# Recutting the head of a fused attention and MLP kernel

## The chip, the cores and the metric

The kernel runs on one core of one Trainium2 chip. The metric is the device time of one execution in microseconds (us); the runs before the change have a median of 356.44 us.

## The reference

Attention over 8 batches and 8 heads, 576 tokens of 64 features, with 16 extra "beacon" keys and values in front that every query sees; the rest is causal. The result, as 4608 tokens of 512 features, goes through a two-layer MLP with a leaky ReLU.

```python
k_all = np.concatenate([beacon_k, k], axis=2)
v_all = np.concatenate([beacon_v, v], axis=2)
scores = (1 / np.sqrt(D)) * np.matmul(q, k_all.transpose(0, 1, 3, 2))
scores = np.where(causal, -1e9, scores)      # causal only among the 576 own keys
a = softmax(scores)
x = np.matmul(a, v_all)                      # (B, H, S, D) -> (B*S, H*D)
h = x @ w_in                                 # 4608 x 512 @ 512 x 2048
out = np.maximum(0.01 * h, h) @ w_out        # 2048 x 512
```

## The kernel before

The work is cut into 32 groups, one for each pair of heads of a batch: group g is pair g % 4 of batch g // 4. Every engine's queue is written out by hand, in the order of the Python code (`tc.manual_schedule`), so each engine runs its instructions strictly in that order, and what the code puts earlier stands earlier in the queue of its engine.

For a group the steps are: queries and keys with features on the partitions (`qT`, `kT`); `score`, in four parts, each of which fills one of two PSUM buffers (`ps_sc`), with ScalarE's exponential behind it into `aT` (three buffers, `a_bufs`); `masks`, four GpSimd selects that clear what lies above the diagonal; `value`, in two halves, the product with v and the division by the row sum (VectorE); and `finish`, five transposes that put the result into `xT`, from which the MLP reads. `value` runs two groups behind `score`, and `finish` three.

The MLP is cut into "groups" of its own: `moe1` (four matmuls of 512 columns, then ScalarE's leaky ReLU into `gT`) and `moe2` (four matmuls of the second layer; every fourth is copied out by VectorE and stored by SP). `fill()` issues the next one whose inputs are there. They fill TensorE between the steps of attention.

The keys and queries come in two ways. For the first two batches (groups 0 to 7) they are loaded by GpSimd's DMA with a cast to bf16 (`load_qk`), turned by TensorE (`t_q`, 18 transposes of 64 x 64 for each of q and k) and copied from PSUM by VectorE or ScalarE. The very first pair is loaded in fp32 by SP and ScalarE (`load_first_pair`) and cast by VectorE and ScalarE (`first_cast`). From batch 2 on, GpSimd permutes them (`permute`), a transposing DMA turns them (`turn_pairs`, on SP's queue) and GpSimd copies them into order (`in_order`, a beacon column block of 16, then q, then k). Each `kT` buffer has 16 beacon columns in front; they are copied from `bkT`, which `beacon_transposes` fills from the cast beacon keys (`cast_beacon_k`). There are two `kT` buffers (`k_bufs`).

v comes in fp32 by SP in five chunks a batch (`load_v`), after the first keys have landed, and is cast by GpSimd (`cast_v`) into `v_aug`. The weights come by GpSimd's DMA with a cast, w_in and w_out in four quarters each, between groups 3 and 6 (`loads`). At the very start TensorE runs 34 matmuls on the identity (`warm_up`).

The main loop `for g in range(NG + 3)` has two forms: groups 0 to 7 (the head) follow a fixed list, with a special stretch at g = 8 that works off what is left of batches 0 and 1, runs 22 MLP groups, and loads batch 2; from there on MLP groups are spread over eight slots in each iteration. Work of GpSimd for later batches is put into `loads(g)`.

Of the kernel before, what the change touches and what calls it, by code (L numbers as in the profile page):

```python
# [15 lines left out]
def kernel(  # L16
# [11 lines left out]
    nc = tc.nc  # L28
# [69 lines left out]
    k_bufs = [singles.tile([128, NKB * 128], BF16, name=f"kT{i}") for i in range(2)]  # L98
# [9 lines left out]
    def load_w_in(i):  # L108
        return nc.gpsimd.dma_start(
            out=w_in_sb[:, :, i * 512 : (i + 1) * 512], in_=w_in_r[:, :, i * 512 : (i + 1) * 512]  # L110
        )

    def load_w_out(i):
        return nc.gpsimd.dma_start(
            out=w_out_sb[:, i * 4 : (i + 1) * 4, :], in_=w_out_r[:, i * 4 : (i + 1) * 4, :]
        )
# [5 lines left out]
    def load_qk(b, grp):  # L122


        qk_raw[b, grp] = (
            qkpool.tile([128, 2, RI, D], BF16, name="q_raw"),
            qkpool.tile([128, 2, RI, D], BF16, name="k_raw"),
        )
        first = None
        for e in range(2):  # L130
            if b == 0 and grp == 0 and e == 0:
                continue
            h0 = 4 * grp + 2 * e
            for src, dst in zip((q, k), qk_raw[b, grp]):
                dma = nc.gpsimd.dma_start(  # L135
                    out=dst[e * RP : (e + 1) * RP],
                    in_=src[b, h0 : h0 + 2].rearrange("h (p i) d -> p h i d", i=RI),
                )
                first = first or dma
        return first  # L140
# [3 lines left out]
    def load_first_pair():  # L144
        load_beacon_k(0, 1, nc.scalar)
        t = rawpool.tile([128, NKB, H, D], FP32, name="v_raw")
        flat = t[0:RP].rearrange("p c h d -> p (c h d)")
        n = 2 * RI * D
        for i in range(2):
            first_raw.append(flat[:, i * n : (i + 1) * n].rearrange("p (h i d) -> p h i d", h=2, i=RI))  # L150
        for eng, src, dst in zip((nc.sync, nc.scalar), (q, k), first_raw):
            last = eng.dma_start(out=dst, in_=src[0, 0:2].rearrange("h (p i) d -> p h i d", i=RI))
        return last

    first_cast = [singles.tile([RP, 2, RI, D], BF16, name=f"{n}_cast") for n in "qk"]
# [26 lines left out]
    def beacon_transposes(b0, b1):  # L182
# [6 lines left out]
        for par in range(2):  # L189
            ps_ = slice(par * 64, par * 64 + 64)  # L190
            nc.vector.tensor_copy(
# [35 lines left out]

    def t_q(g, which, copy=nc.vector.tensor_copy):
# [4 lines left out]
        if which == 0:  # L233
            dst = headpool.tile([128, S], BF16, name="qT")
            qk[g] = [dst]
        else:
            kT = k_bufs[g % 2]
            nc.vector.tensor_copy(out=kT[:, 0:NB], in_=bkT[:, b, hp])
            qk[g].append(kT)
            dst = kT[:, NB : NB + S]  # L240
# [28 lines left out]
    def in_order(g):  # L269
# [4 lines left out]
        kT = k_bufs[g % 2]  # L274
# [11 lines left out]
    def score(g, n):  # L286
# [21 lines left out]
        )  # L308

# [130 lines left out]
    def warm_up(n):  # L440

        ps = ps_one.tile([128, 512], FP32, name="av", tag="one")
        for i in range(n):
            nc.tensor.matmul(out=ps[:, 0:128], lhsT=ident, rhs=ident, start=True, stop=True)
# [15 lines left out]
    with order:  # L460
# [4 lines left out]
        load_beacon_k(1, B, nc.sync)  # L465
        load_v(0, after=first)
        load_v(1)
        make_pads()
        make_ones()
        cast_beacon_k(0, 1, nc.scalar.copy)  # L470
        nc.vector.tensor_copy(out=first_cast[0], in_=first_raw[0])
        nc.scalar.copy(out=first_cast[1], in_=first_raw[1])
        cast_beacon_k(1, B, nc.gpsimd.tensor_copy)
        cast_v(0, nc.gpsimd, 0, 1)
        load_qk(1, 0)
        cast_v(0, nc.gpsimd, 1, 3)
        warm_up(34)
        beacon_transposes(0, 1)
        t_q(0, 0)
        t_q(0, 1, nc.scalar.copy)  # L480

        def loads(g):
            b, hp = divmod(g, NPAIR)
            if g == 1:
                cast_v(0, nc.gpsimd, 3, 5)
            elif g == 2:
                load_qk(1, 1)
            elif g == 3:
                cast_v(1, nc.gpsimd, 0, 3)
                load_w_in(0)  # L490
            elif g == 4:
                cast_v(1, nc.gpsimd, 3, 5)
                load_w_in(1)
                load_w_in(2)
            elif g == 5:
                load_w_in(3)
                load_w_out(0)
                load_w_out(1)
            elif g == 6:
                load_w_out(2)  # L500
                load_w_out(3)
            elif g == 7:
                load_qk(2, 0)
            elif g >= 2 * NPAIR:
                if has(g + 1):
# [28 lines left out]
        for g in range(NG + 3):  # L534
# [3 lines left out]
            if g < 2 * NPAIR:  # L538
# [3 lines left out]
                if has(g - 3):  # L542
                    finish(g - 3)
                if g == 2:
                    beacon_transposes(1, B)
                if g + 1 < 2 * NPAIR:
                    t_q(g + 1, 0)
                    t_q(g + 1, 1, nc.scalar.copy if g in (4, 6) else nc.vector.tensor_copy)
                if g > 2:
                    value(g - 2, 0)  # L550
                if g == 7:
                    fill()
                score(g, 2)
                score(g, 3)
                if g == 2:
                    value(0, 0)
                if g >= 6:
                    fill()
                if has(g - 2):
                    value(g - 2, 1)  # L560
                masks(g)
                continue

            if g == 2 * NPAIR:
# [6 lines left out]
                load_v(2)  # L571
                in_order(g)
                cast_v(2, nc.gpsimd)
# [85 lines left out]
```

The softmax here doesn't subtract the row's maximum and nothing guards it: scores larger than these inputs give would overflow.

## Time and profile before

| what | value |
|---|---|
| median of 4 runs | 356.44 us (355.56 to 357.4) |
| profiled execution, its own time | 356.41 us |
| span of that execution, first to last instruction | 354.7 us |
| busy: TensorE | 341.0 us (96%) |
| busy: ScalarE | 189.1 us (53%) |
| busy: GpSimd | 202.0 us (57%) |
| busy: VectorE | 92.8 us (26%) |
| mean granted TensorE clock | 0.980 |
| first exponential starts | 8.77 us |
| first exponential of group 7 starts | 37.14 us |
| block of 22 MLP groups starts | 48.42 us |

PE is TensorE's matmuls, PEld its weight loads, DVE is VectorE, ACT ScalarE, POOL GpSimd, SP SyncE; ACTq, SPq and POOLq are the queues on which DMAs are issued. A row of the timeline gives start and duration in us, engine, line, operation, output and inputs, how many, and in brackets how long the engine was idle before it and what ended that. In a row of stages the numbers behind the window are the window's length and then, for each engine, busy us and the number of instructions; then the granted clock as a share of full speed, the busy share of the DMA engines and what they moved.

### The profile page before, as it was taken

How to read it: one execution, taken by the hardware profiler on the slowest of the kernel's cores; microseconds unless marked ns; L12 is line 12 of the kernel's file. 1: busy time of each engine (PE TensorE's matmuls, PEld its weight loads, DVE VectorE, ACT ScalarE, POOL GpSimd, SP SyncE). 2: the span in 40 equal slices, each digit the busy share in tenths (PEclk: the TensorE clock that was granted, in tenths of full speed). 3: DMA queues.
4: the chain of work that ended last, by engine and by line, in shares of the span. 5: the costliest groups of instructions: out<-in, count | busy, mean ns of one | idle time of the engine just before them, and what ended most of it. 6: DMA issues, size and time to landing. Idle time of an engine off the chain costs nothing.

```text
span 354.7 us, 7340 instructions
## 1 busy us (share of the span) xinstructions
PE 341.0 (96%) x3002; PEld 173.1 (49%) x3002; DVE 92.8 (26%) x231; ACT 189.1 (53%) x278; POOL 202.0 (57%) x343
## 2 busy tenths in 40 slices
PE   6899999998899999999999999999999999999996
PEld 5566554443454454444444454444444554444444
DVE  2478420002233223222222223222322241000111
ACT  3969754576455873478337843685358403633300
POOL 6699927399899899957695769574431100000000
PEclk9579999999999999999999999999999999999999
DMA  8999999997797976991589356900110011000012
GB/s 170 209 198 161 194 204 187 224 217 124 163 198 114 174 146 125 136 234 31 97 148 225 56 98 114 177 2 1 61 59 2 0 62 59 2 30 30 31 60 88
DMA packets 86929, 40.87 MB, mean 115 GB/s; under 512 B 69872, under 2 KB 82160, under 8 KB 86896
## 3 DMA queue, kind: packets, MB, share of 16 engines
q1 hardware_dynamic: 73456, 26.75, 35.2%
q0 software_dynamic: 13152, 13.34, 24.8%
q8 instruction: 23, 0.38, 0.5%
q10 hardware_dynamic: 288, 0.33, 0.4%
q14 instruction: 10, 0.08, 0.1%
HBM read 37.22 MB, written 9.44 MB: 132 GB/s over the span
## 4 chain that ended last, share of the span: by engine, by line
PE 73%; DMA 11%; POOL 9%; issue 2%; DVE 2%; SPq 1%; ACT 1%; POOLq 0%; ACTq 0%
PE acc L409 32%; PE acc L387 27%; PE av L351 7%; PE sc L297 6%; DMA v_raw<-in_v_dram 4%; DMA w_out_sb<-in_moe_w_out_dram 4%; POOL aT L320 3%; DMA q_raw<-in_q_dram 2%; PE tp L373 2%; DMA v_raw<-in_k_dram 1%; POOL v_aug L224 1%; DVE osb L418 1%; POOL qT L277 1%; POOL kT L277 1%; POOL k_raw L135 1%
## 5 line engine op out<-in xcount | busy, mean ns | idle before, releaser
L387 PE MATMUL acc<-xT,w_in_sb 128*128 128x512 bf16 x576 | 140.2, 379 | 1.4 <-DVE xT L378 1.4
L409 PE MATMUL acc<-w_out_sb,gT 128*128 128x512 bf16 (+1 forms) x592 | 139.6, 374 | 0.0
L306 ACT ACTIVATE aT<-sc 128x1024 bf16<-128x1024 f32 (+3 forms) x128 | 104.2, 869 | 64.7 <-PE sc L297 63.3
L394 ACT ACTIVATE gT<-acc 128x512 bf16<-128x512 f32 x144 | 85.9, 601 | 79.2 <-PE acc L387 79.2
L409 PEld LDWEIGHTS <-gT 128*128 128x128 bf16 x592 | 53.3, 98 | 58.7 <-issue 6.1
L320 POOL TENSOR_SCALAR_AFFINE_SELECT aT<-aT 128x384 bf16<-128x384 bf16 (+2 forms) x128 | 52.5, 448 | 50.2 <-PE av L351 40.3
L387 PEld LDWEIGHTS <-w_in_sb 128*128 128x128 bf16 x576 | 51.9, 98 | 59.5 <-issue 4.2
L418 DVE COPY osb<-acc 128x512 f32<-128x512 f32 (+1 forms) x37 | 25.1, 677 | 134.7 <-PE acc L409 134.6
L351 PEld LDWEIGHTS <-aT 128*128 128x128 bf16 (+1 forms) x960 | 37.5, 99 | 14.7 <-issue 2.6
L297 PE MATMUL sc<-qT,kT 64*128 64x80 bf16 (+4 forms) x384 | 37.1, 295 | 5.5 <-POOL kT L277 2.4
L351 PE MATMUL av<-v_aug,aT 128*128 128x65 bf16 (+1 forms) x960 | 40.7, 196 | 0.0
L361 DVE TENSOR_TENSOR x_nat<-av,rec 128x384 bf16<-128x384 f32 x64 | 31.4, 491 | 2.2
L224 POOL CAST v_aug<-v_raw 128x512 bf16<-128x512 f32 (+1 forms) x40 | 23.3, 616 | 9.6 <-DMA v_raw<-in_v_dram 9.5
L297 PEld LDWEIGHTS <-kT 64*128 64x128 bf16 x384 | 12.9, 96 | 31.3 <-issue 18.7
L277 POOL COPY qT<-q_turn 128x576 bf16<-128x576 bf16 x24 | 28.1, 1171 | 0.0
L277 POOL COPY kT<-k_turn 128x576 bf16<-128x576 bf16 x24 | 28.0, 1167 | 0.0
L378 DVE COPY xT<-tp 128x576 bf16<-128x576 bf16 x32 | 14.5, 455 | 50.9 <-PE tp L373 50.9
L360 DVE RECIPROCAL rec<-av 128x6 f32<-128x6 f32 x64 | 12.0, 187 | 59.2 <-PE av L351 59.2
L135 POOL DMA_DIRECT2D k_raw<-in_k_dram x31 | 19.6, 632 | 4.6 <-DMA w_out_sb<-in_moe_w_out_dram 3.9
L135 POOL DMA_DIRECT2D q_raw<-in_q_dram x31 | 19.0, 613 | 2.7 <-DMA w_out_sb<-in_moe_w_out_dram 2.5
L164 POOL COPY q_nat<-q_raw 128x1152 bf16<-128x1152 bf16 x12 | 13.7, 1145 | 5.5 <-DMA q_raw<-in_q_dram 5.4
L373 PEld LDWEIGHTS <-x_nat 128*128 128x128 bf16 (+2 forms) x160 | 11.2, 98 | 8.8 <-DVE x_nat L361 1.7
(36 smaller groups left out, 85.0 us busy)
## 6 DMA issues: line engine op xcount, KB each, us to landing
out_dram<-osb SPq DMA_DIRECT2D x35, 256.0 KB, 2.3
v_raw<-in_v_dram SPq DMA_DIRECT2D x24, 256.0 KB, 5.1
q_raw<-in_q_dram POOLq DMA_DIRECT2D x31, 144.0 KB, 5.1
k_raw<-in_k_dram POOLq DMA_DIRECT2D x31, 144.0 KB, 5.4
w_in_sb<-in_moe_w_in_dram POOLq DMA_DIRECT2D x4, 512.0 KB, 7.9
w_out_sb<-in_moe_w_out_dram POOLq DMA_DIRECT2D x4, 512.0 KB, 13.1
v_raw<-in_v_dram SPq DMA_DIRECT2D x8, 224.0 KB, 3.6
v_raw<-in_v_dram SPq DMA_DIRECT2D x8, 160.0 KB, 5.0
```

The costliest lines, as they stand in the source:

```text
L135: dma = nc.gpsimd.dma_start(out=dst[e * RP : (e + 1) * RP], in_=src[b, h0 : h0 + 2].rearrange("h (p i) d -> p h i d", i=RI),)
L224: eng.tensor_copy(out=dst[0 : ROWS[c], c, :, 0:D], in_=t[0 : ROWS[c], c])
L277: nc.gpsimd.tensor_copy(out=dst.rearrange("c (p i) -> c p i", i=RI), in_=t[:, :, e].rearrange("c i p -> c p i"),)
L297: nc.tensor.matmul(out=sc[:, par, col - c0 : col - c0 + w], lhsT=kT[ps_, c * 128 : (c + 1) * 128], rhs=qT[ps_, q0 : q0 + w], start=True, s ...
L306: nc.scalar.activation(out=aT[:, :, c0 : c0 + w], in_=sc[:, :, 0:w], func=AF.Exp, scale=0.125)
L320: nc.gpsimd.affine_select(out=part, in_=part, compare_op=ALU.is_ge, fill=0.0, base=base, channel_multiplier=-1, pattern=pattern,)
L351: nc.tensor.matmul(out=avv[:, n, 0 : D + 1], lhsT=aT[0 : ROWS[c], par, a0 : a0 + 128], rhs=va[0 : ROWS[c], c, 2 * hp + par, :], start=(c = ...
L361: nc.vector.tensor_tensor(out=x_nat[:, t0:t1].rearrange("p t e d -> p (t e) d"), in0=avv[:, :, 0:D], in1=rec[:, n0:n1, None].to_broadcast( ...
L387: nc.tensor.matmul(out=acc, lhsT=w_in_sb[:, j, fc * 128 : (fc + 1) * 128], rhs=xT[:, j, i * 512 : (i + 1) * 512], start=(j == 0), stop=(j ...
L394: nc.scalar.activation(out=gT[i][:, fc, :], in_=acc, func=AF.Prelu, alpha=0.01)
L409: nc.tensor.matmul(out=acc[:, 0:w], lhsT=gT[i][:, fc, t * 128 : (t + 1) * 128], rhs=w_out_sb[:, fc, c0 : c0 + w], start=(fc == 0), stop=(f ...
L418: nc.vector.tensor_copy(out=osb[:, 0:w], in_=acc[:, 0:w])
```

## The change

- ScalarE's queue issues the first keys' DMA first and the beacon keys' DMA second; that load takes two batches instead of one. The other six are loaded by SP behind v of batch 1, cast by GpSimd in group 6, and transposed at g = 8.
- The first keys are cast half by ScalarE and half by VectorE, into buffers of the pool for q_nat and k_nat; the beacon's cast, transposes, and columns for groups 0 and 1 stand ahead of these casts.
- The 34 identity matmuls become 24, 12, 6 and 10, spread over the start, and 12 in each of groups 0 and 1.
- In the head, `score` parts 0 and 1 are followed at once by the next group's transposes, and `finish` goes to the end of the iteration. MLP groups are taken out of group 6; one is in group 7, and one more in front of g = 8.
- The beacon columns of groups 2 to 7 are copied by GpSimd instead of VectorE; there are three `kT` buffers.
- Group 0 is masked by VectorE, by multiplying with a triangle of ones that GpSimd makes once.
- v of batch 0 is cast earlier in GpSimd's queue; loads of q and k of batch 1 are cut by pair and issued a little later; each weight comes in two halves, issued in groups 4 to 6.
- `in_order(9)` moves from `loads(8)` to g = 8, ahead of `cast_v(2)`.

```diff
-    k_bufs = [singles.tile([128, NKB * 128], BF16, name=f"kT{i}") for i in range(2)]
+    k_bufs = [singles.tile([128, NKB * 128], BF16, name=f"kT{i}") for i in range(3)]
...
+    def load_w_in(half):
+        cols = slice(half * DF // 2, (half + 1) * DF // 2)
+        return nc.gpsimd.dma_start(out=w_in_sb[:, :, cols], in_=w_in_r[:, :, cols])
+
+    def load_w_out(half):
+        rows = slice(half * NF // 2, (half + 1) * NF // 2)
+        return nc.gpsimd.dma_start(out=w_out_sb[:, rows, :], in_=w_out_r[:, rows, :])
...
     def load_first_pair():
-        load_beacon_k(0, 1, nc.scalar)
...
             last = eng.dma_start(out=dst, in_=src[0, 0:2].rearrange("h (p i) d -> p h i d", i=RI))
+        load_beacon_k(0, 2, nc.scalar)
         return last
...
+    def beacon_columns(g, eng):
+        b, hp = divmod(g, NPAIR)
+        eng.tensor_copy(out=k_bufs[g % 3][:, 0:NB], in_=bkT[:, b, hp])
...
-            kT = k_bufs[g % 2]
-            nc.vector.tensor_copy(out=kT[:, 0:NB], in_=bkT[:, b, hp])
+            kT = k_bufs[g % 3]
...
+    tri = singles.tile([128, 128], BF16, name="tri")
+
+    def make_tri():
+
+        nc.gpsimd.memset(tri, 1.0)
+        nc.gpsimd.affine_select(out=tri, in_=tri, compare_op=ALU.is_ge, fill=0.0,
...
+    def masks_by_tri(g):
+
+        aT = probs[g]
+        diag = aT[:, :, 512 : 512 + 3 * 464].rearrange("p e (c x) -> p e c x", c=3)[:, :, :, 0:128]
+        for part, seen in (
+            (aT[:, :, 0:112], tri[:, None, NB:128].to_broadcast([128, 2, 112])),
+            (diag, tri[:, None, None, :].to_broadcast([128, 2, 3, 128])),
+            (aT[0:80, :, 1648:1728], tri[0:80, None, 0:80].to_broadcast([80, 2, 80])),
+        ):
+            nc.vector.tensor_tensor(out=part, in0=part, in1=seen, op=ALU.mult)
...
+    def keep_busy(n):
+
+        if not busy:
+            busy.append(ps_one.tile([128, 512], FP32, name="av", tag="one"))
+        for i in range(n):
+            nc.tensor.matmul(out=busy[0][:, 0:128], lhsT=ident, rhs=ident, start=True, stop=True)
...
-        load_beacon_k(1, B, nc.sync)
         load_v(0, after=first)
         load_v(1)
+        load_beacon_k(2, B, nc.sync)
         make_pads()
+        cast_beacon_k(0, 2, nc.scalar.copy)
+        keep_busy(24)
+        beacon_transposes(0, 2)
+        beacon_columns(0, nc.vector)
+        beacon_columns(1, nc.vector)
+        nc.vector.tensor_copy(out=first_cast[0], in_=first_raw[0])
+        nc.scalar.copy(out=first_cast[1][:, 0], in_=first_raw[1][:, 0])
+        nc.vector.tensor_copy(out=first_cast[1][:, 1], in_=first_raw[1][:, 1])
+        keep_busy(12)
+        t_q(0, 0)
+        keep_busy(6)
+        t_q(0, 1, nc.scalar.copy)
+        keep_busy(10)
+        make_tri()
         make_ones()
-        cast_beacon_k(0, 1, nc.scalar.copy)
-        nc.vector.tensor_copy(out=first_cast[0], in_=first_raw[0])
-        nc.scalar.copy(out=first_cast[1], in_=first_raw[1])
-        cast_beacon_k(1, B, nc.gpsimd.tensor_copy)
-        cast_v(0, nc.gpsimd, 0, 1)
-        load_qk(1, 0)
-        cast_v(0, nc.gpsimd, 1, 3)
-        warm_up(34)
-        beacon_transposes(0, 1)
-        t_q(0, 0)
-        t_q(0, 1, nc.scalar.copy)
+        beacon_columns(2, nc.gpsimd)
+        cast_v(0, nc.gpsimd, 0, 2)
+        load_qk(1, 0, (0,))
+        cast_v(0, nc.gpsimd, 2, 5)
 
         def loads(g):
             b, hp = divmod(g, NPAIR)
...
+            if g in (2, 3, 4, 5, 6):
+                beacon_columns(g + 1, nc.gpsimd)
+            if g == 2:
+                load_qk(1, 0, (1,))
+                load_qk(1, 1, (0,))
             elif g == 3:
+                load_qk(1, 1, (1,))
+            elif g == 4:
+                load_w_in(0)
                 cast_v(1, nc.gpsimd, 0, 3)
-                load_w_in(0)
-            elif g == 4:
+            elif g == 5:
+                load_w_in(1)
                 cast_v(1, nc.gpsimd, 3, 5)
...
                 load_w_out(0)
+            elif g == 6:
                 load_w_out(1)
...
+                cast_beacon_k(2, B, nc.gpsimd.tensor_copy)
             elif g == 7:
                 load_qk(2, 0)
             elif g >= 2 * NPAIR:
-                if has(g + 1):
+                if has(g + 1) and g > 2 * NPAIR:
                     in_order(g + 1)
...
                 score(g, 0)
                 score(g, 1)
-                if has(g - 3):
-                    finish(g - 3)
-                if g == 2:
-                    beacon_transposes(1, B)
                 if g + 1 < 2 * NPAIR:
                     t_q(g + 1, 0)
-                    t_q(g + 1, 1, nc.scalar.copy if g in (4, 6) else nc.vector.tensor_copy)
-                if g > 2:
+                    t_q(g + 1, 1, nc.scalar.copy if g in (3, 5) else nc.vector.tensor_copy)
+                    if g == 1:
+                        masks_by_tri(0)
+                else:
+                    fill()
+                if g >= 3:
                     value(g - 2, 0)
-                if g == 7:
-                    fill()
                 score(g, 2)
                 score(g, 3)
+                if g < 2:
+                    keep_busy(12)
                 if g == 2:
-                    value(0, 0)
-                if g >= 6:
-                    fill()
-                if has(g - 2):
+                    value(g - 2, 0)
+                if g >= 2:
                     value(g - 2, 1)
-                masks(g)
+                if g >= 3:
+                    finish(g - 3)
+                if g > 0:
+                    masks(g)
                 continue
...
                 load_v(2)
+                fill()
+                beacon_transposes(2, B)
                 in_order(g)
+                in_order(g + 1)
                 cast_v(2, nc.gpsimd)
```

## The prediction

> **What bounds the kernel now.** I read the page first, then busy time by stage, then the timeline of the first 110 us, then the waits of TensorE.
>
> ```profile
> PE 341.0 (96%) x3002; PEld 173.1 (49%) x3002; DVE 92.8 (26%) x231; ACT 189.1 (53%) x278; POOL 202.0 (57%) x343
> ```
>
> TensorE is busy 341.0 of 354.7 us, so only some 14 us of idle time, and work done at a low clock, can be won. The stages (us, then busy us and instructions of PE, PEld, DVE, ACT, POOL, then the granted clock, DMA share, GB/s) show where:
>
> ```profile
> 0.00:8.77 8.77, 5.38 (x75) 4.58 (x75) 2.42 (x13) 3.37 (x4) 6.09 (x15) 1.00 0.85 169
> 8.77:22.77 14.00, 12.71 (x215) 8.40 (x215) 7.08 (x16) 11.21 (x14) 9.98 (x20) 0.51 1.17 204
> 22.77:36.65 13.88, 12.74 (x310) 9.31 (x305) 10.35 (x27) 12.56 (x18) 13.88 (x28) 1.00 1.06 176
> 36.65:48.42 11.77, 11.20 (x154) 6.83 (x151) 5.81 (x17) 7.05 (x12) 8.47 (x18) 1.00 1.22 196
> 48.42:87.00 38.58, 38.58 (x229) 17.07 (x227) 4.25 (x9) 23.42 (x36) 26.56 (x41) 1.00 1.06 190
> 87.00:97.50 10.50, 8.15 (x77) 3.66 (x75) 2.85 (x7) 4.34 (x6) 8.96 (x13) 1.00 0.81 170
> ```
>
> From 48.42 TensorE has no gap until 87; at 87 to 97.5 it loses 2.35 us. Before 36.65 the exponentials (ACT) and GpSimd are as full as TensorE, and from 8.8 to 22.8 TensorE runs at half clock. So there are two places: the head, up to 48.42 (where the block of 22 MLP groups begins), and the two gaps near 90. Behind both, TensorE's work is the same in both kernels, so what it gains there lasts to the end.
>
> The head's start, and the two gaps, in the timeline (start, us, engine):
>
> ```profile
> 0.84 0.39 ACTq L172 DMA_DIRECT2D bk_raw<-in_beacon_k_dram  x1
> 1.27 0.72 ACTq L152 DMA_DIRECT2D v_raw<-in_k_dram  x1
> 1.43 3.81 PE L444 MATMUL av<-ident 128*128 128x128 bf16 x34 [1.43 <-POOL ident masks.py:199]
> 2.59 0.30 ACT L177 CAST bk<-bk_raw 128x128 bf16<-128x128 f32 x1 [0.50 <-DMA bk_raw<-in_beacon_k_dram]
> 4.62 0.75 DVE L471 CAST q_cast<-v_raw 64x1152 bf16<-64x1152 f32 x1 [3.28 <-DMA v_raw<-in_q_dram]
> 5.93 1.15 ACT L472 CAST k_cast<-v_raw 64x1152 bf16<-64x1152 f32 x1 [3.05 <-DMA v_raw<-in_k_dram]
> 7.64 0.93 POOL L177 CAST bk<-bk_raw 128x896 bf16<-128x896 f32 x1 [1.67 <-DMA bk_raw<-in_beacon_k_dram]
> 8.77 3.16 ACT L306 ACTIVATE aT<-sc 128x1024 bf16<-128x1024 f32 x4 [0.49 <-PE sc L297]
> ...
> 88.87 0.58 PE L297 MATMUL sc<-qT,kT 64*128 64x512 bf16 x4 [1.40 <-POOL kT L277]
> 96.53 0.59 PE L297 MATMUL sc<-qT,kT 64*128 64x512 bf16 x4 [0.95 <-POOL kT L277]
> ```
>
> The first exponential runs at 8.77, behind key load, cast, transposes and copy. Both gaps are TensorE waiting for keys that GpSimd puts in order.
>
> **The change, part by part.**
>
> *The start.* The keys' DMA takes the beacon's place on ScalarE's queue: 0.43 us earlier (1.27 to 0.84), landing near 5.5 instead of 5.91. The key cast is halved: 1.15 us becomes 0.58 on ScalarE beside some 0.38 on VectorE (half of the 0.75 above). Together this would bring the first exponential some 1 us forward. But the beacon load now stands behind the keys, is twice as large, and its cast is the first thing in ScalarE's queue; behind it wait the beacon transposes, and behind those, on VectorE, two bkT copies, two beacon columns, and only then the query cast. In the trace the beacon load behind the queries on SP's queue landed at 7.64, 3.0 us after them, for 224 KB. Scaled to 64 KB that is 0.86 us behind the keys; if it overtook them it could land by 4, some 2 us after its issue at 1.56 as the beacon did here. The Trainium skill ("DMA: Bandwidth & Descriptors", section "Two DMAs through the same engine are not ordered") says that descriptors of one queue start in order but are pipelined: a small load does not overtake by much, but need not wait out its whole length. This speaks against the change. I take 0.4 us: beacon at 5.9. Then: cast 0.42 (0.30 for half the size) 6.35; two transposes 0.4, 6.75; two copies 0.45 (two of half the size took 0.39) 7.2; two columns of 0.16, 7.5; query cast 0.75, 8.25; key half 0.38, 8.65; query transposes 0.57, 8.8; six filler matmuls of 0.106 (34 took 3.6) 9.45; key transposes 0.47 and copy 0.64, 10.55; score to exponential 0.43: first exponential at 11.0, **2.3 later**. By the row's full 0.86 it is 11.5; with an early beacon 9.2.
>
> *The seven iterations to group 7.* Before, 28.4 us (8.77 to 37.14, the first exponential of group 7): 4.05 each, where four exponentials take 3.26 back to back ("ACT L306" at 27.69). The excess is half clock, the seven beacon transposes (0.93 at 16.11), value(0) waiting for v casts, and finish between the scores, which delays score(2): 0.47 us idle on ACT at 31.42. After: finish goes behind value; beacon transposes go to group 8; masks of group 0 leave GpSimd for three VectorE products (an estimate of 1.3 us for their 1152 elements, from the 0.49 for 384 of x_nat; they stand between the copies of groups 2 and 3, and VectorE was busy 7.1 of 14 us there; uncovered they would cost those 1.3 once). Groups 0 to 2 take 3.3 each, groups 3 and 5 with a key copy on ACT (0.61) 3.85, 4 and 6 some 3.5 (score(g+1) behind value and finish: 3.26 plus 0.2): 24.6. Filler in groups 0 and 1 costs nothing at full clock (ACT covers it) and at half clock up to 12 x 0.106 = 1.3 us each, beside 3.1 of cold work; I add 0.5 for both. Sum 25.1, **3.3 less**, so group 7 begins at 36.1, 1.0 before its former time.
>
> GpSimd must keep up, as score(g) now waits for a beacon column in its queue. From masks(1) on: masks 1.6 each, columns 0.15 (0.14 to 0.20 in rows), four and two q/k issues 2.4 and 1.2, weight issues 0.76, five v casts 3.0. From the end of the v casts to column 7 that is 17.6 us. Those casts, waiting for v that is issued 0.45 earlier and not behind 224 KB of beacon, end near 16.4, and masks(1) waits for exp(1,3) near 18; column 7 comes near 34.6, before 35.6. It hides, with 1 us to spare; the mask triangle (0.2 + 0.3) and column 2 lie in GpSimd's former wait of 3.54 us for v. Were v as late as before (19.67), column 7 would come at 37.3 and group 7 start 1.7 later.
>
> *From group 7 to the 22 groups.* Before 11.77 us. After, with as many MLP groups (seven), it has six beacon transposes (0.36) and one more finish (0.3) and waits 0.5 for exp(7,1) before score 3, against 0.57 of idle before: 12.3. And one MLP group (0.87) is still owed, since one ran in group 6 before. **1.4 more.**
>
> Head: 2.3 - 3.3 + 1.4 = +0.4.
>
> *Weights in halves.* Eight issues of 0.76 become four; the lanes of q/k loads of batch 2 come free earlier (before, POOL waited 7.1 us on them, from 42 to 53). The first half (1.05 MB) is issued near 26.3; at 200 GB/s (the rate at 45 to 55) and 2 us, it lands near 34, and the first MLP group wants it at 36. Cost nothing, cover 2 us. The later beacons, now behind v(1) on SP and cast in group 6 (0.93), are wanted only by in_order(8) near 58. The q/k loads of group 5 move from 12.7 behind masks(1), to about 19; transposes of group 5 want them near 25.5, and the median landing is 6.0: cover about 0.5, uncovered up to 1.
>
> *Batch 2.* in_order(9), 2.5 us, moves ahead of cast_v(2), where GpSimd waited 3.47 us for v anyway. Its chain behind is 2 us or more earlier, worked through row by row with the masks and q/k issues in their order: in_order(11) ends by 86.8 instead of 88.85 (TensorE wants it at 88.87 - 1.40 = 87.5), in_order(12) by 94.5 instead of 96.5 (wanted at 96.53 - 0.95 - 1.40 = 94.2). It is possible because k_bufs has three. Up to 2.35; with 0.3 of wait left, **-2.1**. What is late next is in_order(13) and (14), which had 0.4 us of slack; they move as well.
>
> Sum: +0.4 - 2.1 = -1.7, from the profiled execution's own 356.41 (its span 354.7 and 1.7 around it), to 354.7. The median of the runs is 356.44, the same.
>
> **The clock.** In half-microsecond windows the granted clock is 0.50 from 9.1 to 22.8, though 34 filler matmuls stood ahead (their 0.106 each is slow too, though the record says 1.00 there). The new filler (24 + 12 + 6 + 10, and twice 12) is spread out. The skill's "TensorE: Matmul & The Clock Gate", Part 1 (the HAM clock gate), lets the clock rise only after a window of 3.4 us of activity; the first 24 last only 2.5 us and are followed by 2.3 us of idle, so by the rule the start stays cold, while 6.4 to 13 is full: I take warm from about 13. By the trace alone (full clock first at 22.8) groups 0 to 2 would take 4.2 each instead of 3.5 with filler: the sum would be 356.9.
>
> **The rivals.**
> - *Beacon early or clock up early*: first exponential at 9.2 to 10, GpSimd's column 7 then the limit; the head starts group 7 another 1.1 earlier, total 353.6. For it: small load. Against: queue order. Chance 0.13.
> - *Cold to 22.8*: +2.2, 356.9. For it: what the trace did after as much filler. Against: TensorE had idle and few full-size matmuls in those windows, and now has filler. Chance 0.14.
> - *The first weight half is late.* In the trace quarters took 6.8 to 9.0 us to land, w_out quarters up to 15. If the half takes 15 it lands at 41.3; TensorE, in order, stands at the first group from 36.1, and all behind: +5.2, less 0.8 of waits that hide in it: +2.7 in all, 359.1. It is slower than before from a landing 12.3 us after its issue (38.6), measurably from 13.4. Against: v is out of the way by then. Chance 0.10.
> - *The gaps near 90 stay* (the chain is held by the q/k loads instead, which took 7 us to land; GpSimd waited 0.74 and 1.53 for them): 356.8. Chance 0.08.
> - My forecast, 353.4 to 356.2: 0.55.
>
> **How the numbers follow.** A measurement here tells 0.3% (1.07 us) from no change. Faster: 0.46 of my 0.55, the 0.13 and a little of the others: 0.60. Slower: 0.08 of the late half, 0.08 of the cold and the gap case, 0.02 of my own: 0.18. Same: 0.22. The range takes in the cold head and the standing gaps, and leaves out most of the late half and a head that gains 1.8 more than mine: 352.9 to 357.6.
>
> **What would show it.** First exponential near 11, group 7's near 36, 22 groups from 48.0; no TensorE wait on kT at 85 to 97; clock back before 14. It is wrong if the first exponential is before 9.5, if TensorE waits for w_in, or if the wait on kT returns.

## Result and the profile after

The changed kernel takes 357.82 us in the median of 43 runs (356.4 to 360.88), the kernel before 356.44 beside it (62 runs). The ratio is 1.0038, with a 95% interval of 1.0026 to 1.005: **1.4 us slower, where 354.7 and 1.7 faster was forecast.** Ratios, here and below, leave out the few executions more than 1.5% above the fastest of their kernel; medians and counts do not.

The profiled execution of the changed kernel took 356.40 us of its own, span 354.7. That is the fastest of its 43 runs and almost exactly the profiled time of the kernel before (356.41); so the trace explains a draw, and the last 1.4 us have to be found by experiments. The page's first row, and then the same six stages as before (us; busy us and instructions of PE, PEld, DVE, ACT, POOL; granted clock; DMA share; GB/s):

```profile
PE 342.9 (97%) x3044; PEld 175.3 (49%) x3044; DVE 93.2 (26%) x230; ACT 188.5 (53%) x278; POOL 198.7 (56%) x343
...
0.00:8.77 8.77, 4.28 (x38) 3.89 (x38) 1.54 (x14) 2.26 (x3) 5.50 (x17) 1.00 0.83 163
8.77:22.77 14.00, 13.00 (x223) 8.86 (x221) 6.49 (x12) 9.24 (x12) 6.86 (x14) 1.00 1.17 207
22.77:36.65 13.88, 12.85 (x335) 9.58 (x331) 9.81 (x24) 13.14 (x18) 13.41 (x30) 1.00 0.97 152
36.65:48.42 11.77, 11.69 (x181) 7.88 (x178) 7.99 (x24) 7.83 (x12) 9.66 (x21) 1.00 1.14 194
48.42:87.00 38.58, 38.58 (x230) 17.12 (x228) 3.58 (x7) 23.90 (x37) 26.14 (x40) 1.00 1.09 205
87.00:97.50 10.50, 10.28 (x91) 4.75 (x88) 3.81 (x9) 4.90 (x8) 9.40 (x14) 1.00 0.62 122
```

Read the last stage first: TensorE is busy 10.28 us instead of 8.15, so the two gaps near 90 gave 2.13 back, as forecast. Then ScalarE in the second stage: 9.24 us of work instead of 11.21. The exponentials start later, and that is where the 2.13 went again. The start in the timeline (start, us, engine, line, operation, count, and the idle time before it with what ended it):

```profile
0.84 0.74 ACTq L150 DMA_DIRECT2D v_raw<-in_k_dram  x1
1.61 0.84 ACTq L177 DMA_DIRECT2D bk_raw<-in_beacon_k_dram  x1
6.78 0.41 ACT L182 CAST bk<-bk_raw 128x256 bf16<-128x256 f32 x1 [4.69 <-DMA bk_raw<-in_beacon_k_dram]
7.09 0.67 ACT L512 CAST k_nat<-v_raw 64x576 bf16<-64x576 f32 x1
7.24 0.40 PE L191 MATMUL tp<-ident,bk 128*128 128x128 bf16 x2 [3.06 <-ACT bk L182]
7.67 0.46 DVE L196 COPY bkT<-tp 64x128 bf16<-64x128 bf16 x2 [6.30 <-PE tp L191]
8.16 0.25 DVE L235 COPY kT<-bkT 128x16 bf16<-128x16 bf16 x2
8.33 0.74 DVE L511 CAST q_nat<-v_raw 64x1152 bf16<-64x1152 f32 x1
9.13 0.69 PE L255 MATMUL tp<-ident,q_nat 64*64 64x64 bf16 x18 [0.21 <-DVE q_nat L511]
9.75 0.82 PE L481 MATMUL av<-ident 128*128 128x128 bf16 x6
11.12 1.25 PE L481 MATMUL av<-ident 128*128 128x128 bf16 x10
12.96 3.35 ACT L314 ACTIVATE aT<-sc 128x1024 bf16<-128x1024 f32 x4 [1.08 <-PE sc L305]
```

One chain can be read downwards: beacon landing, beacon cast, beacon transposes, two copies, two columns, and only at 8.33 the cast of queries, which the casts-first kernel below could start at 4.64 (the kernel before at 4.62). The first exponential runs at 12.96, where before it ran at 8.77 and the forecast had 11.0.

In the rows around group 7 and the block of 22 MLP groups (first matmul of the block at 49.86, 48.42 before) the head comes out 2.3 us longer: 1.44 later, and one MLP group of 0.87 still owed. With 2.13 won near 90 that is +0.2, which is why the two profiled times agree.

### The profile page after: what moved, and what is told of

Read it like the earlier page. It is cut to its first block, busy times and chain, and to the rows that moved or that the text cites. A ratio compares the mean times of both kernels' runs of the same rounds, so it can differ in the third digit from the quotient of the medians.

```text
span 354.7 us, 7391 instructions
## 1 busy us (share of the span) xinstructions
PE 342.9 (97%) x3044; PEld 175.3 (49%) x3044; DVE 93.2 (26%) x230; ACT 188.5 (53%) x278; POOL 198.7 (56%) x343
## 4 chain that ended last, share of the span: by engine, by line
PE 77%; DMA 9%; POOL 5%; DVE 3%; ACT 3%; issue 2%; SPq 1%; POOLq 0%; ACTq 0%
PE acc L443 32%; PE acc L421 27%; PE sc L305 7%; PE av L385 7%; DMA q_raw<-in_q_dram 4%; ACT aT L314 2%; DMA k_raw<-in_k_dram 2%; DMA v_raw<-in_v_dram 2%; DMA bk_raw<-in_beacon_k_dram 1%; PE tp L407 1%; DVE osb L452 1%; PE av L481 1%; PE tp L255 1%; POOL aT L354 1%; DVE xT L412 1%
## 5 line engine op out<-in xcount | busy, mean ns | idle before, releaser
L354 POOL TENSOR_SCALAR_AFFINE_SELECT aT<-aT 128x224 bf16<-128x224 bf16 (+1 forms) x124 | 50.9, 449 | 49.4 <-PE av L385 37.0
L452 DVE COPY osb<-acc 128x512 f32<-128x512 f32 (+1 forms) x37 | 25.1, 678 | 136.9 <-PE acc L443 136.8
L169 POOL COPY q_nat<-q_raw 128x1152 bf16<-128x1152 bf16 x12 | 13.8, 1147 | 7.8 <-DMA q_raw<-in_q_dram 7.8
```

What stands on the lines that cost most here:

```text
L354: nc.gpsimd.affine_select(out=part, in_=part, compare_op=ALU.is_ge, fill=0.0, base=base, channel_multiplier=-1, pattern=pattern,)
L452: nc.vector.tensor_copy(out=osb[:, 0:w], in_=acc[:, 0:w])
```

## Experiments

Eleven kernels, each with the kernel before run beside it on the same chip. Ratios are to that kernel, with 95% intervals; 0.001 is 0.36 us.

| kernel | median us (runs) | ratio |
|---|---|---|
| changed kernel | 357.82 (43) | 1.0038 [1.0026, 1.005] |
| beacon load first | 355.37 (13) | 0.9971 [0.9948, 0.9995] |
| first casts ahead of the beacon's | 355.26 (22) | 0.9970 [0.9953, 0.9986] |
| no late filler | 356.66 (22) | 1.0006 [0.9993, 1.002] |
| move of `in_order(9)` undone | 360.25 (9) | 1.0094 [1.0061, 1.0127] |
| kernel before, with the move alone | 355.60 (22) | 0.9976 [0.9958, 0.9994] |
| q and k loads ahead of permutes | 356.57 (22) | 1.0000 [0.9985, 1.0015] |
| weights in quarters | 358.29 (7) | 1.0067 [1.0035, 1.0099] |
| casts first, filler whole | 354.44 (7) | 0.9923 [0.9896, 0.9951] |
| the same, q and k ahead of permutes | 354.13 (6) | 0.9907 [0.9872, 0.9941] |
| the same, weights in quarters | 355.15 (22) | 0.9975 [0.9961, 0.9989] |
| move alone, q and k ahead of permutes | 354.76 (22) | 0.9963 [0.9942, 0.9984] |

### Is it the beacon's place? Two ways to take it off the path

In the changed kernel the beacon stands behind the keys as a load and ahead of them as work. The first experiment undoes the one, the second the other.

```diff
     def load_first_pair():
+        load_beacon_k(0, 2, nc.scalar)
...
-        load_beacon_k(0, 2, nc.scalar)
         return last
```

> The changed kernel with the beacon load first on ScalarE's queue again, still two batches of it. Theory 1 (the head's start is late since the beacon lands at 6.7, behind the keys, and the query and key casts stand behind its chain): beacon lands near 3.3, first exponential at 9.5 to 10.3 instead of 12.96, group 7 near 36.3, time 355.4, some 2.4 below the changed kernel. Theory 2 (the filler matmuls at half clock, in front of work that is ready, make the loss): first exponential still after 11, time 357. Theory 3 (the loop of the head itself, with finish at its end and columns by GpSimd, is slower): start earlier, but group 7 still at 38, time 357.5.

```diff
+        nc.vector.tensor_copy(out=first_cast[0], in_=first_raw[0])
+        nc.scalar.copy(out=first_cast[1][:, 0], in_=first_raw[1][:, 0])
+        nc.vector.tensor_copy(out=first_cast[1][:, 1], in_=first_raw[1][:, 1])
         cast_beacon_k(0, 2, nc.scalar.copy)
         keep_busy(24)
-        beacon_transposes(0, 2)
-        beacon_columns(0, nc.vector)
-        beacon_columns(1, nc.vector)
...
         t_q(0, 1, nc.scalar.copy)
+        beacon_transposes(0, 2)
+        beacon_columns(0, nc.vector)
+        beacon_columns(1, nc.vector)
```

> The changed kernel with the same loads, but the casts of the first queries and keys, and their transposes, ahead of the beacon's cast, transposes and columns on every engine. Theory 1, second half (not the landing alone but the place ahead of the casts costs): beacon still lands at 6.7, but is wanted last, first exponential near 9.3 and time near 355.2. If the landing alone is the cost: first exponential at 11.5 to 12, time 357.

Both come out 2.4 us below the changed kernel (0.9971 and 0.9970 against 1.0038). In the second the load stays where the change put it, and the beacon still lands late: ScalarE casts it at 7.13. Its first exponential is at 9.32 instead of 12.96. (Its profiled execution took 358.82 us, 3.6 above the median; where that comes from is shown below, at 97 us, so only the head is read from it here.) First the beacon-first kernel, then the casts-first one:

```profile
2.81 0.41 ACT L182 CAST bk<-bk_raw 128x256 bf16<-128x256 f32 x1 [0.71 <-DMA bk_raw<-in_beacon_k_dram]
8.45 3.16 ACT L314 ACTIVATE aT<-sc 128x1024 bf16<-128x1024 f32 x4 [0.49 <-PE sc L305]
```

```profile
5.95 0.67 ACT L507 CAST k_nat<-v_raw 64x576 bf16<-64x576 f32 x1 [3.86 <-DMA v_raw<-in_k_dram]
7.13 0.40 ACT L182 CAST bk<-bk_raw 128x256 bf16<-128x256 f32 x1 [0.50 <-DMA bk_raw<-in_beacon_k_dram]
9.32 3.36 ACT L314 ACTIVATE aT<-sc 128x1024 bf16<-128x1024 f32 x4 [1.25 <-PE sc L305]
```

So it is not the load's place in the queue that costs, but that everything else was queued behind work that needs it. Nor does the early start hang on TensorE's clock: in the kernel below that has casts first and the filler in one piece, the 18 transposes of the first queries take 0.69 us instead of the 0.47 of full rate, and the first exponential is at 9.36 all the same.

Note what an earlier start is worth. The beacon-first kernel starts its exponentials 4.5 us earlier than the changed one, but group 7 only 1.8 earlier (its scores at 36.41, not 38.25). Two things take the rest in this execution. The loop runs into what had been in time, here a beacon column of group 3 and the keys of group 4:

```profile
18.84 0.59 PE L305 MATMUL sc<-qT,kT 64*128 64x512 bf16 x4 [0.44 <-POOL kT L235]
21.06 0.47 PE L255 MATMUL tp<-ident,k_raw 64*64 64x64 bf16 x18 [1.24 <-DMA k_raw<-in_k_dram]
```

And the clock, at full rate from about 6, is lost again: the record has 0.50 from 23 to 29, which makes 0.75 of the stage:

```profile
22.77:36.65 13.88, 13.31 (x266) 9.45 (x263) 9.07 (x23) 11.18 (x15) 13.51 (x29) 0.75 1.15 188
```

By their scores, group 3 takes 4.79 us there (with the wait of 1.24 in it) and group 4 takes 5.31, where the changed kernel, by then at full rate, takes 3.64 and 3.55. The forecast had sized covers for group 5's keys (0.5 us) and group 7's column (1 us), and none for these two.

### Does the spread filler help?

```diff
-        keep_busy(12)
         t_q(0, 0)
-        keep_busy(6)
         t_q(0, 1, nc.scalar.copy)
-        keep_busy(10)
...
-                if g < 2:
-                    keep_busy(12)
```

> The changed kernel with the first 24 filler matmuls alone; the 12, 6 and 10 at the start and the 12 in groups 0 and 1 are left out. Theory 1: the beacon still lands at 6.7; first exponential only 0.7 earlier, at 12.3; groups 0 and 1 shorter by up to 1 us in sum if the clock is no colder: time 356.5 to 357. Theory 2: first exponential near 11.5 and 2.5 us off the time, 355.3. If the filler does what it is there for and warms the clock, leaving it out makes the low clock last longer, past 20 us, and the time is the same or up to 1 us more: 358.5.

1.2 us less in the medians, 1.1 by the ratios. The first exponential comes at 11.81. First the changed kernel's TensorE in groups 0 and 1, then the one without late filler:

```profile
15.22 1.46 PE L481 MATMUL av<-ident 128*128 128x128 bf16 x12
16.62 0.99 PE L305 MATMUL sc<-qT,kT 64*128 64x512 bf16 x4
19.41 0.84 PE L481 MATMUL av<-ident 128*128 128x128 bf16 x12
20.19 0.69 PE L305 MATMUL sc<-qT,kT 64*128 64x512 bf16 x4
```

```profile
11.15 0.99 PE L305 MATMUL sc<-qT,kT 64*128 64x512 bf16 x4 [0.74 <-ACT kT L258]
14.67 1.11 PE L305 MATMUL sc<-qT,kT 64*128 64x512 bf16 x4 [0.53 <-ACT aT L314]
18.30 1.11 PE L305 MATMUL sc<-qT,kT 64*128 64x512 bf16 x4 [0.65 <-ACT aT L314]
22.98 0.99 PE L305 MATMUL sc<-qT,kT 64*128 64x512 bf16 x4
```

The counts and durations give the clock: 12 identity matmuls take 1.46 at 15.22 and 0.84 at 19.41, so the changed kernel runs at half rate until about 19, and the other until about 23. The filler does bring the clock up sooner: in all six traces with the spread filler it is up by 19 (with the beacon first at 6, to be lost again at 23), while in all seven without it the scores run at half rate up to 21.5 or longer.

What that is worth can be read from the starts of the scores. Group 0 takes 4.32 us with filler (12.30 to 16.62) and 3.52 without, group 1 takes 3.57 and 3.63. But group 2, where the first value product joins, takes 3.61 with filler and 4.68 without, still at half rate, and group 3 takes 3.64 and 3.86. So in the loop the filler gives back 0.55 us more than it costs. The loss lies in front of the loop, where the 12, 6 and 10 stand before and between the transposes and ahead of the first score: with them the first exponential comes 1.15 us later, though the beacon's cast is 0.12 earlier (6.78, not 6.90). Up to group 7 the difference is 0.61 us (37.64, not 38.25), less than the 1.1 between the ratios; these two traces do not show the rest.

### What is the move of in_order(9) worth?

```diff
                 in_order(g)
-                in_order(g + 1)
                 cast_v(2, nc.gpsimd)
...
-                if has(g + 1) and g > 2 * NPAIR:
+                if has(g + 1):
                     in_order(g + 1)
```

> The changed kernel with in_order(9) back in loads(8), so the recut head with the old place of that step. In the changed kernel's profile in_order(11) ended at 89.08, as late as before (88.81), since batch 2's loads were later; TensorE came 2 us later and waited 0.23. If the move was still worth its 2.5 us of GpSimd's queue there, undoing it brings in_order(11) to 91.5 and a wait of over 2: time 359.9, the head alone then costs 3.5. If the head's cost simply adds to what the move alone gave (0.8 between the medians), 358.6.

The changed kernel without the move takes 360.25; by the ratios the move is worth 2.0 us here, and the rest of the change costs 3.4 (1.0094). Both TensorE waits are back, and longer in sum (2.84 us after 2.35 in the kernel before; a third of 0.53 stands at 74.96). The head has made GpSimd's chain later, and the second wait also has a late load in it, as the next section shows:

```profile
89.69 0.58 PE L305 MATMUL sc<-qT,kT 64*128 64x512 bf16 x4 [1.09 <-POOL kT L285]
99.02 0.59 PE L305 MATMUL sc<-qT,kT 64*128 64x512 bf16 x4 [1.75 <-POOL kT L285]
```

The other way round, the kernel before with the move and what the move needs (third `kT` buffer, first casts in the pool's buffers):

```diff
-    k_bufs = [singles.tile([128, NKB * 128], BF16, name=f"kT{i}") for i in range(2)]
+    k_bufs = [singles.tile([128, NKB * 128], BF16, name=f"kT{i}") for i in range(3)]
...
                 in_order(g)
+                in_order(g + 1)
                 cast_v(2, nc.gpsimd)
...
-                if has(g + 1):
+                if has(g + 1) and g > 2 * NPAIR:
```

> The kernel before with nothing but the move of in_order(9) to g = 8, ahead of cast_v(2), the third kT buffer that it needs, and the first casts in the pool's buffers so that it fits. All theories put the loss of the change into the head, which is as before here: the gaps of 1.40 and 0.95 us at 88.9 and 96.5 go, TensorE idles under 0.4 us there, time 354.3 (2.1 below before). Rival: what is won near 90 is given back later (a wait on GpSimd's keys or on the loads of a later batch): 356.4.

Its profiled execution gains the whole 2.1 (354.33 of its own against 356.41), and TensorE is busy 10.28 of the 10.50 us; but it is almost the fastest of its 22 runs (354.32). The median gains 0.9 (0.2 to 1.5), less than expected: something still takes a good part of it in a typical run.

### What holds GpSimd's chain in a typical run?

GpSimd permutes q and k (L169) when they have landed, and `in_order` stands behind. The row of the second pair's permute near 90, in the changed kernel and in the one with the move undone:

```profile
90.18 1.15 POOL L169 COPY q_nat<-q_raw 128x1152 bf16<-128x1152 bf16 x1 [1.10 <-DMA q_raw<-in_q_dram]
```

```profile
92.84 1.15 POOL L169 COPY q_nat<-q_raw 128x1152 bf16<-128x1152 bf16 x1 [3.21 <-DMA q_raw<-in_q_dram]
```

The same load keeps GpSimd waiting 1.10 us in one execution and 3.21 in another. In the casts-first kernel's execution it is 4.14, and there one can see such a wait arrive at TensorE, by way of the `in_order` behind it:

```profile
89.74 1.15 POOL L169 COPY q_nat<-q_raw 128x1152 bf16<-128x1152 bf16 x1 [4.14 <-DMA q_raw<-in_q_dram]
97.44 0.93 PE L305 MATMUL sc<-qT,kT 64*128 64x512 bf16 x4 [3.60 <-POOL kT L285]
```

This one execution is 3.6 us above its kernel's median, so it shows the path of the wait, not how often it comes. So I issued the second load of a batch ahead of the permutes of the first:

```diff
+                        if hp == 1:
+                            load_qk(b + 1, 1)
                         if hp < 3:
                             for which in range(2):
                                 permute(b + 1, hp - 1, which)
-                        if hp == 1:
-                            load_qk(b + 1, 1)
-                        else:
+                        if hp > 1:
```

> The changed kernel with the second q/k load of each batch from batch 3 on issued ahead of the two permutes (2.3 us earlier on GpSimd's queue), nothing else. Theory: GpSimd's chain near 90 hangs on the landing of that load (q_nat waited 1.10 at 90.18, 4.14 in another run), so the chain is 1 to 2 us earlier, TensorE's waits there shrink in the slower executions: 357.0. Rival: the head alone makes the loss and the chain is covered: 357.8, as the changed kernel.

356.57: 1.25 us below the changed kernel, more than expected. Its profiled execution took 356.47, close to its median, and has no TensorE wait from 85 to 105, with the scores of group 7 at 38.55, so with the changed kernel's head. The edit acts on nothing but when q and k of batches 3 and later are loaded. So a typical run of the changed kernel contains 1.25 us of waiting for them that its profiled one, the fastest, does not have. No trace of the changed kernel itself shows such a run: that its waits lie near 90 is inferred from the rows above.

In the kernel before with the move, the same edit gives 0.9963 after 0.9976, a difference inside the intervals:

> The kernel before, with in_order(9) moved (three kT buffers, first casts in pool buffers) and the second q and k loads of a batch issued ahead of the permutes; the head is that of the kernel before. Theory (typical runs of the moved version still wait near 90 for kT, held up by the landing of q and k; the head recut is worth 1.5 once casts stand first and the filler is whole): 354.6 to 355.2, so 0.5 to 1 above the best version with the recut head (354.1). Rival (the recut head is worth nothing even when mended; all the gain is near 90): 354.1 or less.

Its profiled execution took 357.52, 2.8 above its median, without a wait near 90: there the granted clock is at 0.50 from about 26.5 to 33.5, and the scores of group 7 begin at 40.38 (36.86 with the move alone). Landing times are thus not the only thing that varies from run to run.

### Do the weights in halves cost anything?

```diff
-    def load_w_in(half):
-        cols = slice(half * DF // 2, (half + 1) * DF // 2)
+    def load_w_in(i):
+        cols = slice(i * 512, (i + 1) * 512)
...
                 load_w_in(0)
+                load_w_in(1)
```

(and so on for the other three halves, each split in its place)

> The changed kernel with the weights in quarters again, each issued where its half was. Theory (the halves hold the queue of the batch-2 loads longer: the last k load was issued at 55.03 instead of 53.02, behind a half of w_out): with quarters the last q and k loads of batch 2 are issued one by one as quarters land, the last of them near 54, GpSimd's chain near 90 comes about 1 us earlier, and where the halves cost a kT wait near 90 it goes: 357.2 to 357.6 against 357.8 for the changed kernel. Rival 1 (the halves cost nothing, only the late issue counts): no change, 357.8, last k load at 55. Rival 2 (four more issues of 0.76 on GpSimd in groups 4 to 6 delay masks and beacon columns): group 7 begins 0.5 to 1 later, 358.3 or more.

358.29, not below the changed kernel (and not clearly above it, as the intervals overlap). The profiled execution is the slowest of the seven, 360.30. The first rows are the weight waits of the changed kernel's last two batch-2 loads, then come those of the quarters, and the beacon column of group 7 in the quarters:

```profile
49.09 0.59 POOL L134 DMA_DIRECT2D q_raw<-in_q_dram  x1 [2.78 <-DMA w_out_sb<-in_moe_w_out_dram]
55.03 0.59 POOL L134 DMA_DIRECT2D k_raw<-in_k_dram  x1 [5.34 <-DMA w_out_sb<-in_moe_w_out_dram]
```

```profile
50.39 0.61 POOL L134 DMA_DIRECT2D k_raw<-in_k_dram  x1 [1.45 <-DMA w_out_sb<-in_moe_w_out_dram]
52.90 0.59 POOL L134 DMA_DIRECT2D q_raw<-in_q_dram  x1 [1.90 <-DMA w_out_sb<-in_moe_w_out_dram]
55.43 0.59 POOL L134 DMA_DIRECT2D k_raw<-in_k_dram  x1 [1.94 <-DMA w_out_sb<-in_moe_w_out_dram]
...
40.68 0.58 PE L305 MATMUL sc<-qT,kT 64*128 64x512 bf16 x4 [1.15 <-POOL kT L235]
```

Quarters do shorten the waits for the queue (5.3 us in sum instead of 8.1). But of their issues six instead of three stand ahead of the column that score(7) needs (4.52 us of GpSimd's time instead of 2.44), and TensorE waits 1.15 us for it. Rival 2 fits. In the mended kernel below it shows again, with 1.83 us of waiting, and with 355.15 against 354.13, where the intervals are apart. (The two profiled executions do not differ, 354.93 and 354.90, with group 7's scores at 37.07 and 37.04: in the one with halves the clock came up only after 26, in the other at 21.5.)

> The best version so far (first casts ahead of the beacon's work, filler of 34 at the start, q and k loads ahead of permutes), with the weights in quarters. Theory as for the quarters alone (the queue comes free piece by piece): 353.8 to 354.1. Rival 1 (halves cost nothing): 354.1. Rival 2 (four more issues on GpSimd delay the columns): 354.5 or more.

### A version that beats both

Casts first (the edit above), the filler once as 34 at the start, and then also q and k ahead of the permutes. The edit of the filler:

```diff
-        keep_busy(24)
-        keep_busy(12)
+        keep_busy(34)
         t_q(0, 0)
-        keep_busy(6)
...
-        keep_busy(10)
...
-                if g < 2:
-                    keep_busy(12)
```

> Casts ahead of the beacon's work, and the filler matmuls once more in one run of 34 ahead of the first transposes, none later. If the filler costs (as its absence gave 1.2 in the changed kernel): groups 0 and 1 take 3.6 instead of 4.3, time 354.6, 0.7 below the version with filler. If the spread filler helps once the casts are first: 355.5.

> The last one with the second q/k load of a batch ahead of the permutes as well. Both causes taken away: time 353.9, the fastest of all, about 2.5 below the kernel before; no wait of TensorE on kT near 90. If the chain near 90 is covered anyway: as the last one.

354.44 and 354.13 us, 0.8% and 0.9% below the kernel before, in seven and six runs. By the ratios the whole filler gains 1.7 us on casts first with the spread one, more than forecast, and the traces do not show why: both start their first scores at 8.7, and it is the spread filler that reaches group 7 first (35.68, not 36.63), as its clock is up by 19 and the other's only near 26. That cause stays open. In the second kernel, the first exponential is at 9.75, TensorE has no wait of 0.2 us or more between 17 and 50, and the last stage is full:

```profile
87.00:97.50 10.50, 10.50 (x92) 4.94 (x90) 3.66 (x8) 6.09 (x8) 10.50 (x20) 1.00 0.66 116
```

Its ratio of 0.9907 stands against 0.9963 for the old head with the same two GpSimd edits, where the intervals all but touch. The recut loop, once its start is mended, is probably worth something, but these runs do not settle how much, and its parts were not run one by one.

## Why the prediction was wrong, step by step

**The start** is the step that failed: "first exponential at 11.0, 2.3 later", measured 12.96, 4.2 later. Of the 2.0 us between them, 0.9 were there when the beacon's cast began, at 6.78 instead of 5.9: v's load, which waits for the keys, was issued at 5.86, so the keys came 0.4 later than taken (issued 0.43 earlier than in the kernel before, they landed hardly sooner: v's load was issued at 5.92 there, so v's "0.45 earlier" did not happen either), and the beacon 0.9 behind them instead of 0.4. The row of the trace had scaled to 0.86; the prediction leaned on the Trainium skill instead ("DMA: Bandwidth & Descriptors", "Two DMAs through the same engine are not ordered") and took 0.4. The measurement decides for the row. That rule says what may complete before what, not how long a small load takes behind a large one. The other 1.1 us lie in the chain behind it: six filler matmuls of 0.82, not 0.64 (the row of 34 says 3.81, not the 3.6 that the sum used), transposes of 0.69 at half rate, not 0.57 and 0.47, and 1.09 instead of 0.43 between the end of the key copy (11.87) and the exponential, since the last ten filler matmuls, which the sum left out, held the first score until 12.30, and the score ran at half rate.

**The seven iterations** were sized well: 25.78 us (first exponential of group 0 at 12.96 to that of group 7 at 38.74), forecast 25.1, before 28.4. The three mask products, estimated at 1.3 from a row whose 0.49 is the mean of two shapes (384 elements take 0.56), took 0.88. The missing 0.7 is in groups 0 and 1, which took 4.32 and 3.57 by their scores; "I add 0.5 for both" to 3.3 each was 1.3.

**The clock**: "warm from about 13" failed. It was about 19 in the profiled execution. The Trainium skill's page on the clock gate ("TensorE: Matmul & The Clock Gate", Part 1) also says that the window runs freely and that the cold count varies from run to run, and the forecast had left that part out; here the same head is warm by 15.16 with the move undone, at about 17.5 with the weights in quarters, and near 19 in the changed kernel and in the one with earlier q and k loads. The rival "cold to 22.8" had the right direction. The forecast's "full clock first at 22.8" misread the kernel before, however. Its first score ran at full rate and its second at half:

```profile
8.34 0.59 PE L297 MATMUL sc<-qT,kT 64*128 64x512 bf16 x4 [0.74 <-ACT kT L250]
11.44 1.11 PE L297 MATMUL sc<-qT,kT 64*128 64x512 bf16 x4 [0.34 <-ACT aT L306]
```

So after its 34 filler matmuls the clock had come up, and it was lost again at 9, as it was at 22.5 with the beacon first. In these executions a clock that was up did not stay up, and the forecast counted on it from 13 on.

**From group 7 to the 22 groups** was better than forecast: 11.61 us instead of 12.3, with one MLP group of 0.87 owed, as said. The head's sum is 4.2 - 2.6 + 0.7 = +2.3, and +0.4 was forecast. These 1.9 us put the profiled execution 1.7 above the forecast; the median lies another 1.4 above that, which is the matter of the gaps near 90 below.

**Batch 2** had the right mechanism and size, 2.13 in the stage near 90 for "-2.1". But the sentence "its chain behind is 2 us or more earlier" does not hold on the clock: `in_order(11)` ended at 89.08, before at 88.81. The forecast took the chain's former times as given. They hang on the head, however: GpSimd issued the first weights at 29.35 (before 26.75, forecast 26.3) and the last batch-2 keys at 55.03 (before 53.02), so the move only made up for what the head lost. In the kernel before, with the move alone, `in_order(11)` ends at 86.91, as forecast.

**Weights in halves**: "cost nothing" is right on balance, as far as the quarters' loss tells, but that the lanes "come free earlier" is wrong: GpSimd waited 8.1 us for them, where it had been 7.1. The first MLP group started at 38.91 without a wait, so the rival of a late half did not happen.

**Columns**: the "1 us to spare" for column 7 was 0.2: the copy ended at 38.02 and the scores began at 38.25. This held only because the head was late and the weights had four issues instead of eight.

**The gaps near 90** as a rival had 0.08. The profiled execution shows them gone (0.23 us of wait), but the median, by the run with earlier q and k loads, still contains some 1.2 us of that kind. The forecast took one execution's landing times for those of all.

## What to carry to other kernels

When a load is moved behind another, look for the work that waits for it and ask what stands behind that work in each in-order queue: here moving the casts of queries and keys ahead of the beacon's work gave back 2.4 us with the load left where it was. When an early stage is shifted, shift with it every issue that its helper engine makes for later stages, before counting a gain there. And a gap that a DMA's landing sets should be sized from several executions, not from one.

## What was not expected of the hardware

- A load of 64 KB issued 0.8 us behind the keys' on the same queue was ready 0.9 us after them; issued first, a load of the same size was ready at 2.81. On its own it is quick, and behind the keys it takes the keys' time and more.
- The granted clock in the record is 1.00 in the changed kernel's first stages, and 1.00 throughout in the one without late filler, while identical matmuls ran at half rate there (0.99 to 1.11 us for the four score matmuls that take 0.58 to 0.59 later). In the kernel before the same matmuls, equally slow, are recorded at 0.51. At the start of these executions, durations of known matmuls told the clock where the record did not.
- The same head came to lasting full rate at about 15 us in one execution, 17.5 in another and near 19 in two more. A full clock was also lost again: the record has 0.50 from 23 to 29 with the beacon first, while TensorE was busy 13.31 of 13.88 us in that stage.
